# Folded groups 165 rows apart, small slots for the last raw rows, and a value test in flat parts, in a channel-attention kernel

## The chip, the cores and the metric

The kernel runs on one core of a Trainium2 chip. The metric is the device time of one execution in microseconds (us). Five engines take part: TensorE (PE, the sums), VectorE (DVE, bit work and scaling), ScalarE (ACT, the sigmoid, a range test, and the queue that issues all stores), SyncE (SP, the queue that issues all loads), and GpSimd (POOL, a fallback that does no work on these inputs). Loads and stores run on the core's 16 DMA engines.

## The reference

```python
H = W = 384
C = 384
x: (1, H, W, C) bf16, normal * 0.05        w1d: (1,) bf16

g = jnp.einsum("bhwc->bc", x) / (H * W)    # mean of each channel
s = sigmoid(g * w1d[0])                    # with k = 1
return x * s[:, None, None, :]
```

Each of the 384 channels is averaged over 147,456 positions, and the whole tensor (113 MB) is then scaled by one factor per channel. No output can be computed before every input has been read, and the tensor is larger than the core's own memory.

## The kernel before

The 147,456 positions are seen as 1152 "rows" of 128 partitions: one row is one position (384 channels, 768 bytes) in each of the 128 partitions, 98 KB in all.

**First pass.** SP loads all 1152 rows into one tile, `arena`, which has 275 row places. PE sums each row over the partitions by a matrix of ones (`sum_rows`, L227), all into one PSUM bank. 799 rows are "streamed": once PE has read them, their places are used again, and they are loaded a second time later. The other 353 rows are kept on the chip until they are scaled:

- 18 rows in PSUM (ACT copies them there, L315);
- 240 rows "folded" in four groups, `QS = [16, 16, 16, 12]`: of each group of 4q rows, q rows (called u) are loaded into the places `U`, 3q rows (called w) into the group's own area, and then the bits of u are put into the top exponent bits of w, so that 4q rows take 3q places;
- 95 rows raw, in `A`, `B`, `C`, `Y`, `U` and `T`, loaded last.

Before a group's w rows come, its area serves as a place for streamed rows; so do A, B and C.

**The fold** (`fold`, pieces of 4 rows of u and 12 of w; four pieces in groups 0 to 2, three in group 3). DVE makes four shifted copies of u in T (four instructions through the helper `bits`, L247), then writes the twelve w rows and the four u rows, masked and XORed, to Y for a range test (L247 again, one instruction for all of w, `three(ya, p)`, and one for u), then puts the copies into w (two through `join`, L253). The joins wait until PE has summed the rows that they change. ACT then reads Y in place and takes its sum into `seen` (L289). So the next piece's writes to Y wait for ACT, the next group's load into U waits for the last piece's reads of U, and the load of the raw rows into Y waits for ACT's last pass. If any tested value is out of range, `verdict` and `again` recompute the folded rows; on these inputs they do nothing.

**Order of the loads.** SP issues the loads in the order in which the program lists them, and a load that must wait for its place holds every later one. Before: the 18 rows, 523 streamed rows through all four areas, group 0, 72 streamed rows, group 1, 72, group 2, 72, group 3, 60, then the 95 raw rows.

**Second pass.** Once all 1152 rows are summed, ACT computes the factors (`s_bf`, L361). DVE scales what is on the chip (`scale`, L370), unfolds the groups (`unfold`), scales the PSUM rows (`from_psum`), and ACT's queue stores them; as places come free, SP loads streamed rows again, which are scaled and stored in turn. A loop at the end of the program plays this through with a row time of 0.2275 us and writes the instructions in the order in which it sees places come free. In the program a load waits for the stores that free its place, whatever the loop had assumed.

`Flow` collects all steps with the rows they read and write, and sets the waits from that; transfers of one queue share 24 semaphores, so that a transfer also waits for the one 24 before it.

Of the kernel before, what the change touches and what calls it, by code (L numbers as in the profile page):

```python
# [128 lines left out]
def kernel(  # L129
# [13 lines left out]
    B, H, W, C = x.shape  # L143
# [12 lines left out]
    base, areas = 0, []  # L156
# [1 line left out]
        areas.append((base, 3 * q))  # L158
        base += 3 * q
    RAW = {}  # L160
    for name, n in (("A", 16), ("B", 16), ("C", 15), ("Y", 16), ("U", 16), ("T", 16)):
        RAW[name] = (base, n)
        base += n
    ROWS = base
# [22 lines left out]
    def view(t, r0, n):  # L187
        return t[r0 * P : (r0 + n) * P, :].rearrange("(p r) c -> p r c", r=n)

    def rows(lo, n):  # L190
        return [("a", r) for r in range(lo, lo + n)]
# [5 lines left out]
    N_STREAM = RPP - kept  # L197
# [8 lines left out]
    c_raw = {}  # L206
# [8 lines left out]
    def load(chunk, a, lo=0, hi=None):  # L215

        r0, n = chunk
        hi = n if hi is None else hi
        fl.add(
            "SP",  # L220
            lambda: nc.sync.dma_start(out=arena[:, a : a + hi - lo, :], in_=view(xf, r0, n)[:, lo:hi, :]),  # L221
            writes=rows(a, hi - lo), dma=True,
        )

    def sum_rows(a, n):
        def emit(i, first, last):
            return nc.tensor.matmul(acc, lhsT=ones[:], rhs=arena[:, i, :], start=first, stop=last)  # L227

        for i in range(a, a + n):
            first, last = summed[0] == 0, summed[0] == RPP - 1  # L230
            fl.add(
                "PE", lambda i=i, f=first, l=last: emit(i, f, l),
                reads=[("a", i), "ones"], writes=["acc"],
            )
            summed[0] += 1

    def take(chunk, a):
        load(chunk, a)
        sum_rows(a, chunk[1])
# [4 lines left out]
    def bits(dst, src, op0, s0, op1, s1, reads, writes):  # L244
        fl.add(
            "DVE",
            lambda: nc.vector.tensor_scalar(out=dst, in0=src, scalar1=s0, scalar2=s1, op0=op0, op1=op1),  # L247
            reads=reads, writes=writes,
        )

    def join(dst, a, b, op, reads, writes):
        fl.add(
            "DVE", lambda: nc.vector.tensor_tensor(out=dst, in0=a, in1=b, op=op), reads=reads, writes=writes  # L253
        )

    def area(g, lo, p):
        a, n = areas[g]
        v = arena[:, a : a + n, :].rearrange("p (j q) c -> p j q c", j=3)[:, :, lo : lo + p, :]
        q = n // 3
        return v.bitcast(u16), [rows(a + j * q + lo, p) for j in range(3)]  # L260

    def flat(a, p):
        return arena[:, a : a + p, :].bitcast(u16)

    def three(a, p):
        return arena[:, a : a + 3 * p, :].rearrange("p (j q) c -> p j q c", j=3).bitcast(u16)

    SHL, SHR, AND, OR, XOR = (
        Op.logical_shift_left, Op.logical_shift_right, Op.bitwise_and, Op.bitwise_or, Op.bitwise_xor,
    )  # L270

    def fold(k):
        g, lo, p = pieces[k]
        w, wc = area(g, lo, p)
        wall = wc[0] + wc[1] + wc[2]
        ua, ta, ya = RAW["U"][0] + lo, RAW["T"][0], RAW["Y"][0]
        u, uc = flat(ua, p), rows(ua, p)
        for i, (op, by, mask) in enumerate(
            ((SHL, 4, 0x7800), (SHL, 8, 0x7800), (SHL, 12, 0x7000), (SHR, 4, 0x0800))
        ):  # L280
            bits(flat(ta + i * p, p), u, op, by, AND, mask, uc, rows(ta + i * p, p))
        bits(three(ya, p), w, AND, 0x7800, XOR, 0x3800, wall, rows(ya, 3 * p))
        bits(flat(ya + 3 * p, p), u, AND, 0x7800, XOR, 0x3800, uc, rows(ya + 3 * p, p))
        join(w, w, three(ta, p), XOR, wall + rows(ta, 3 * p), wall)
        join(w[:, 2], w[:, 2], flat(ta + 3 * p, p), XOR, wc[2] + rows(ta + 3 * p, p), wc[2])
        y = flat(ya, 4 * p)
        fl.add(
            "ACT",
            lambda: nc.scalar.activation(out=y, in_=y, func=ACTF.Copy, accum_out=seen[:, k : k + 1]),  # L289
            reads=rows(ya, 4 * p), writes=rows(ya, 4 * p) + [("seen", k)],  # L290
        )
# [12 lines left out]
    def stream(n, a):  # L304
        take((streamed[0], n), a)
        streamed[0] += n

    A, Bs, Cs, Y, U, T = (RAW[n][0] for n in "ABCYUT")
    take(c_ps, A)
    psflat = arena[:, A : A + PS, :].rearrange("p r c -> p (r c)")  # L310
    for i, bk in enumerate(banks):
        lo, hi = i * BANK, min((i + 1) * BANK, PS * C)
# [4 lines left out]
            ),  # L317
            reads=rows(A, PS), writes=[("bank", i)],
        )
    GAP = [(0, 48), (1, 12), (2, 12)]  # L320
    TAIL = [("A", 16), ("B", 16), ("C", 15), ("A", 13)]
    before = N_STREAM - 3 * 72 - sum(n for _, n in TAIL)
    i = 0
    while before:
        a, n = areas[i % 4]
        n = min(n, before)
        stream(n, a)
        before -= n
        i += 1
    k = 0  # L330
    for g, q in enumerate(QS):
        if g:
            a, n = areas[(g + 1) % 4] if g < 3 else areas[3]
            n = min(n, 48)
            if g < 3:
                stream(n, a)
            else:
                stream(n, a)
            rest = 72 - n
            stream(rest // 2, A)  # L340
            stream(rest - rest // 2, Bs)
        load(c_u[g], U)
        load(c_w[g], areas[g][0])
        sum_rows(U, q)
        sum_rows(areas[g][0], 3 * q)
        while k < len(pieces) and pieces[k][0] == g:
            fold(k)
            k += 1
    for name, n in TAIL:
        stream(n, RAW[name][0])  # L350
    assert streamed[0] == N_STREAM
    for name in "BCAYU":
        take(c_raw[name], RAW[name][0])
    for lo, hi in ((0, 8), (8, 12), (12, 14), (14, 15), (15, 16)):
        load(c_raw["T"], T + lo, lo, hi)
        sum_rows(T + lo, hi - lo)
    assert summed[0] == RPP

    fl.add(
# [143 lines left out]
    landed = deque()  # L503
    free = deque()
# [17 lines left out]
    def release(name):  # L522
        def f():
            if name in extra and extra[name]:
                extra[name] -= 1
                return
            free.append(RAW[name])
        return f

    for lo, hi in ((0, 1), (1, 2), (2, 4), (4, 8), (8, 16)):  # L530
        landed.append((c_raw["T"], T, lo, hi, None))
    for name in "ABCYU":
        n = RAW[name][1]
        landed.append((c_raw[name], RAW[name][0], 0, n, release(name)))
    unfolded = 0
    psum_done = False
    verdict_done = checked = False
# [3 lines left out]
    while True:  # L541

        if dve_at <= now:
# [9 lines left out]
            elif can:  # L553
                kk = unfolded
                g, lo, p = pieces[kk]
# [18 lines left out]
        while waiting and waiting[0][0] <= now:  # L574
            _, n, then = waiting.popleft()
# [5 lines left out]
        while free and todo[0] < N_STREAM and len(loads) < 6:  # L581
            a, n = free.popleft()
            n = min(n, N_STREAM - todo[0])
# [3 lines left out]
            cuts = list(range(0, n, 16)) + [n]  # L587
# [6 lines left out]
        for q in active:  # L594
            q[0][1] -= DT / len(active)
            if q[0][1] <= 0:
                then = q.popleft()[2]
# [41 lines left out]
```

## Time and profile before

| | |
|---|---|
| median of 3 runs | 793.52 us (793.11 to 794.05) |
| the profiled execution | 796.84 us, of which the span of the profile is 795.1 us |
| moved by DMA | 191.79 MB read, 113.25 MB written, 384 GB/s over the span |
| DVE busy | 466.6 us (59%) |
| PE busy | 226.5 us (28%), 1153 matmuls |
| ACT busy | 86.7 us (11%) |
| factors (`s_bf`) computed | at 332.6 us of the span |

The span is counted from the first to the last instruction of the profiled execution. Engine shares are averages over both passes; the first pass ends at 332.6 us, and PE has almost nothing to do after it. The chain of waits is followed back from the last instruction; in it, "SPq" is the load queue, "ACTq" the store queue.

### The profile page before, as it was taken

How to read it: one execution, taken by the hardware profiler on the slowest of the kernel's cores; microseconds unless marked ns; L12 is line 12 of the kernel's file. 1: busy time of each engine (PE TensorE's matmuls, PEld its weight loads, DVE VectorE, ACT ScalarE, POOL GpSimd, SP SyncE). 2: the span in 40 equal slices, each digit the busy share in tenths (PEclk: the TensorE clock that was granted, in tenths of full speed). 3: DMA queues.
4: the chain of work that ended last, by engine and by line, in shares of the span. 5: the costliest groups of instructions: out<-in, count | busy, mean ns of one | idle time of the engine just before them, and what ended most of it. 6: DMA issues, size and time to landing. Idle time of an engine off the chain costs nothing.

```text
span 795.1 us, 2991 instructions
## 1 busy us (share of the span) xinstructions
PE 226.5 (28%) x1153; PEld 122.2 (15%) x1153; DVE 466.6 (59%) x366; ACT 86.7 (11%) x39; POOL 0.2 (0%) x4
## 2 busy tenths in 40 slices
PE   2878888843837667500000000000000000000000
PEld 1444444421413333200000000000000000000000
DVE  0000000493782987299899938997599986374500
ACT  2000000252552555000000000000000000000000
POOL 0000000000000000000000000000000000000000
PEclk9898989875967889855555555555555555555555
DMA  9999999909559497699999999999999999999996
GB/s 356 433 428 437 422 441 428 402 5 411 212 210 419 182 391 312 261 362 426 425 425 430 432 421 429 432 411 420 425 426 422 423 428 428 425 433 432 425 430 296
DMA packets 28623, 305.25 MB, mean 384 GB/s; under 512 B 2880, under 2 KB 3648, under 8 KB 12096
## 3 DMA queue, kind: packets, MB, share of 16 engines
q1 hardware_dynamic: 11376, 191.80, 57.4%
q10 hardware_dynamic: 17232, 113.25, 34.1%
q8 instruction: 9, 0.15, 0.1%
q14 instruction: 6, 0.05, 0.0%
HBM read 191.79 MB, written 113.25 MB: 384 GB/s over the span
## 4 chain that ended last, share of the span: by engine, by line
DMA 51%; DVE 27%; PE 9%; ACT 5%; ACTq 2%; DVEq 0%; issue 0%; SPq 0%
DMA arena<-in_x_dram 27%; DMA out_dram<-arena 24%; DVE arena L370 10%; PE bank L227 9%; DVE arena L247 9%; ACT arena L289 5%; DVE arena L253 4%; DVE arena L404 2%; ACTq L380 2%; DVE arena L442 1%; DVEq L106 0%; SPq L221 0%; ACT s_bf L361 0%; SPq L634 0%; ACTq L112 0%
## 5 line engine op out<-in xcount | busy, mean ns | idle before, releaser
L247 DVE TENSOR_SCALAR arena<-arena 128x1536 uint16<-128x1536 uint16 x180 | 139.7, 821 | 199.1 <-DMA arena<-in_x_dram 150.0
L227 PE MATMUL bank<-arena,ones 128*128 128x384 bf16 x1152 | 226.3, 364 | 106.3 <-DMA arena<-in_x_dram 106.1
L370 DVE TENSOR_TENSOR arena<-arena,s_bf 128x6144 bf16<-128x6144 bf16 (+5 forms) x76 | 198.1, 2665 | 51.6 <-DMA arena<-in_x_dram 31.2
L227 PEld LDWEIGHTS bank<-arena,ones 128*128 128x128 bf16 x1152 | 122.1, 108 | 210.1 <-DMA arena<-in_x_dram 108.0
L253 DVE TENSOR_TENSOR arena<-arena 128x1536 uint16<-128x1536 uint16 (+1 forms) x75 | 95.4, 1272 | 20.9 <-PE bank L227 20.4
L289 ACT ACTIVATE arena<-arena 128x6144 uint16<-128x6144 uint16 x15 | 79.9, 5323 | 222.6 <-DVE arena L247 222.6
L404 DVE TENSOR_TENSOR arena<-arena,s_bf 128x4608 bf16<-128x4608 bf16 x15 | 38.3, 2552 | 0.0
L463 PE MATMUL bank<-odd,ones 128*128 128x1 bf16 x1 | 0.2, 186 | 31.0 <-DVE odd L458 31.0
L298 DVE TENSOR_SCALAR w_sc<-w_bf 128x1 f32<-128x1 bf16 x1 | 0.2, 153 | 14.8 <-DMA w_bf<-in_w1d_dram 14.8
L442 DVE TENSOR_TENSOR arena<-bank,s_bf 128x768 bf16<-128x768 bf16 (+2 forms) x15 | 5.0, 390 | 0.1
L463 PEld LDWEIGHTS bank<-odd,ones 128*128 128x128 bf16 x1 | 0.1, 104 | 31.3 <-DVE odd L458 31.3
L315 ACT COPY bank<-arena 128x512 uint32<-128x512 uint32 (+1 forms) x7 | 3.6, 566 | 5.9 <-DMA arena<-in_x_dram 5.9
L289 ACT ACTIVATION_READ_ACCUMULATOR arena<-arena 128x1 f32 x15 | 2.8, 186 | 0.0
L361 ACT ACTIVATE s_bf<-bank,w_sc 128x384 bf16<-128x384 f32 x1 | 0.6, 582 | 17.2 <-PE bank L227 17.2
L607 ACT ACT_TABLE_LOAD x1 | 1.3, 1283 | 0.7 <-PEq L623 0.7
L295 DVE MEMSET ones<- 128x128 bf16 x1 | 0.2, 165 | 1.0 <-SPq L106 1.0
L467 DVE CAST odd_i<-bank 128x1 int32<-128x1 f32 x1 | 0.2, 158 | 0.3 <-PE bank L463 0.3
L458 DVE TENSOR_SCALAR odd<-worst 128x1 bf16<-128x1 f32 x1 | 0.2, 157 | 0.0
L453 DVE TENSOR_REDUCE worst<-seen 128x1 f32<-128x15 f32 x1 | 0.2, 161 | 0.0
L623 POOL MEMSET const-bfloat16-1.0<- 128x1 bf16 x1 | 0.1, 102 | 0.0
L623 POOL MEMSET const-uint8-127<- 128x1 uint8 x1 | 0.1, 101 | 0.0
L623 POOL MEMSET const-float32-0.0<- 128x1 f32 x1 | 0.1, 99 | 0.2 <-issue 0.2
(1 smaller groups left out, 0.1 us busy)
## 6 DMA issues: line engine op xcount, KB each, us to landing
arena<-in_x_dram SPq DMA_DIRECT2D x21, 4608.0 KB, 20.7
out_dram<-arena ACTq DMA_DIRECT2D x48, 1536.0 KB, 30.7
arena<-in_x_dram SPq DMA_DIRECT2D x29, 1536.0 KB, 11.8
arena<-in_x_dram SPq DMA_DIRECT2D x5, 3456.0 KB, 26.1
out_dram<-arena ACTq DMA_DIRECT2D x15, 1152.0 KB, 27.8
arena<-in_x_dram SPq DMA_DIRECT2D x8, 1440.0 KB, 11.5
out_dram<-arena ACTq DMA_DIRECT2D x7, 1440.0 KB, 22.8
arena<-in_x_dram SPq DMA_DIRECT2D x5, 1728.0 KB, 7.0
```

Source lines behind the costliest of these rows:

```text
L227: return nc.tensor.matmul(acc, lhsT=ones[:], rhs=arena[:, i, :], start=first, stop=last)
L247: lambda: nc.vector.tensor_scalar(out=dst, in0=src, scalar1=s0, scalar2=s1, op0=op0, op1=op1),
L253: "DVE", lambda: nc.vector.tensor_tensor(out=dst, in0=a, in1=b, op=op), reads=reads, writes=writes
L289: lambda: nc.scalar.activation(out=y, in_=y, func=ACTF.Copy, accum_out=seen[:, k : k + 1]),
L315: lambda bk=bk, lo=lo, hi=hi: nc.scalar.copy(bk[:, 0 : hi - lo].bitcast(u32), psflat[:, lo:hi].bitcast(u32)),
L361: lambda: nc.scalar.activation(out=s_bf[:], in_=acc, func=ACTF.Sigmoid, scale=w_sc[:, 0:1]),
L370: lambda: nc.vector.tensor_tensor(out=v, in0=v, in1=s_bf[:, None, :].to_broadcast([P, n, C]), op=Op.mult),
L380: lambda: nc.scalar.dma_start(out=view(of, r0, n)[:, lo:hi, :], in_=arena[:, a : a + hi - lo, :]),
L404: lambda: nc.vector.tensor_tensor(out=wv, in0=wv, in1=s_bf[:, None, None, :].to_broadcast([P, 3, p, C]), op=Op.mult),
L442: lambda sv=sv, dv=dv, by=by: nc.vector.tensor_tensor(out=dv, in0=sv, in1=by, op=Op.mult),
L463: lambda: nc.tensor.matmul(votes, lhsT=ones[:], rhs=odd[:], start=True, stop=True),
L607: nc.scalar.preload_act_table(ACTF.Sigmoid)
```

## The change

Three things are edited. Nothing that is computed changes, and the numbers of streamed, folded and raw rows are the same.

1. **Spacing.** 225 streamed rows come before group 0, 165 between one group and the next (72 before), and 79 after group 3 (60 before). The streamed rows go in pieces of half an area, 24 or 18 rows (48 or 36 before). Between groups they take the areas that hold no folded group yet, and the small slots.
2. **Small slots.** A, B and C become one stretch A of 47 rows, cut into six slots of 8 rows (the last of 7). The last streamed rows and the raw rows are loaded slot by slot, and in the second pass each slot is stored, freed and loaded again by itself. The raw rows that are scaled first are those of the first slot (1, 1, 2 and 4 rows), where before they were T's.
3. **Test in flat parts.** The instruction that writes all twelve w rows of a piece to Y becomes three, one for each stretch of four rows.

```diff
-    for name, n in (("A", 16), ("B", 16), ("C", 15), ("Y", 16), ("U", 16), ("T", 16)):
+    for name, n in (("A", 47), ("Y", 16), ("U", 16), ("T", 16)):
...
-        bits(three(ya, p), w, AND, 0x7800, XOR, 0x3800, wall, rows(ya, 3 * p))
+        for j in range(3):
+            bits(flat(ya + j * p, p), w[:, j], AND, 0x7800, XOR, 0x3800, wc[j], rows(ya + j * p, p))
...
-    GAP = [(0, 48), (1, 12), (2, 12)]
-    TAIL = [("A", 16), ("B", 16), ("C", 15), ("A", 13)]
-    before = N_STREAM - 3 * 72 - sum(n for _, n in TAIL)
-    i = 0
-    while before:
-        a, n = areas[i % 4]
-        n = min(n, before)
-        stream(n, a)
-        before -= n
-        i += 1
+    def stream_all(n, where):
+        i = 0
+        while n:
+            a, m = where[i % len(where)]
+            m = min(n, m)
+            stream(m, a)
+            n -= m
+            i += 1
+
+    def halves_of(*gs):
+        return [(areas[g][0] + h * areas[g][1] // 2, areas[g][1] // 2) for g in gs for h in (0, 1)]
+
+    SMALL = [(A + i, min(8, Y - A - i)) for i in range(0, Y - A, 8)]
+    BEFORE = [
+        (N_STREAM - 79 - 3 * 165, halves_of(1, 2, 3)),
+        (165, halves_of(1, 2, 3) + SMALL),
+        (165, halves_of(2, 3) + SMALL + halves_of(3) + SMALL),
+        (165, halves_of(3) + SMALL * 9),
+    ]
     k = 0
     for g, q in enumerate(QS):
-        if g:
-            a, n = areas[(g + 1) % 4] if g < 3 else areas[3]
-            n = min(n, 48)
-            if g < 3:
-                stream(n, a)
-            else:
-                stream(n, a)
-            rest = 72 - n
-            stream(rest // 2, A)
-            stream(rest - rest // 2, Bs)
+        stream_all(*BEFORE[g])
         load(c_u[g], U)
         load(c_w[g], areas[g][0])
...
-    for name, n in TAIL:
-        stream(n, RAW[name][0])
+    stream_all(79, SMALL)
     assert streamed[0] == N_STREAM
-    for name in "BCAYU":
-        take(c_raw[name], RAW[name][0])
+    first = 4
+
+    def take_part(name, lo, hi):
+        load(c_raw[name], RAW[name][0] + lo, lo, hi)
+        sum_rows(RAW[name][0] + lo, hi - lo)
+
+    for a, n in SMALL[first:] + SMALL[:first]:
+        take_part("A", a - A, a - A + n)
+    for name in "YU":
+        take_part(name, 0, 16)
...
-    for lo, hi in ((0, 1), (1, 2), (2, 4), (4, 8), (8, 16)):
-        landed.append((c_raw["T"], T, lo, hi, None))
-    for name in "ABCYU":
-        n = RAW[name][1]
-        landed.append((c_raw[name], RAW[name][0], 0, n, release(name)))
+    for j, (a, n) in enumerate(SMALL):
+        lo = a - A
+        cuts = [lo, lo + 1, lo + 2, lo + 4, lo + n] if not j else [lo, lo + n]
+        for e, f in zip(cuts, cuts[1:]):
+            then = (lambda a=a, n=n: free.append((a, n))) if f == lo + n else None
+            landed.append((c_raw["A"], A, e, f, then))
+    landed.append((c_raw["T"], T, 0, 8, None))
+    landed.append((c_raw["T"], T, 8, 16, None))
+    for name in "YU":
+        landed.append((c_raw[name], RAW[name][0], 0, 16, release(name)))
```

What this does to the order of the instructions, at three places. In the rows, 384 elements of a partition are one row, so 128x18432 is a load of 48 rows.

The load queue (SP) from group 0 to group 1, before: U and the w rows of group 0, streamed rows, U of group 1 (waiting for DVE), its w rows.

```order
L221 DMA arena<-in_x_dram 128x6144
L221 DMA arena<-in_x_dram 128x18432 [waits f_PE] x2
L221 DMA arena<-in_x_dram 128x4608 [waits f_ACT]
L221 DMA arena<-in_x_dram 128x4608
L221 DMA arena<-in_x_dram 128x6144 [waits f_DVE]
L221 DMA arena<-in_x_dram 128x18432
```

The same stretch after the change:

```order
L221 DMA arena<-in_x_dram 128x6144
L221 DMA arena<-in_x_dram 128x18432
L221 DMA arena<-in_x_dram 128x9216 [waits f_PE] x4
L221 DMA arena<-in_x_dram 128x6912 x2
L221 DMA arena<-in_x_dram 128x3072 [waits f_ACT]
L221 DMA arena<-in_x_dram 128x3072 x3
L221 DMA arena<-in_x_dram 128x384
L221 DMA arena<-in_x_dram 128x6144 [waits f_DVE]
L221 DMA arena<-in_x_dram 128x18432 [waits f_PE]
```

The load that waits for DVE now stands behind 165 streamed rows instead of 72 (48 + 12 + 12).

The load queue from group 3's U to the raw rows in T, before:

```order
L221 DMA arena<-in_x_dram 128x4608 [waits f_DVE]
L221 DMA arena<-in_x_dram 128x13824
L221 DMA arena<-in_x_dram 128x6144
L221 DMA arena<-in_x_dram 128x6144 [waits f_PE]
L221 DMA arena<-in_x_dram 128x5760 [waits f_PE]
L221 DMA arena<-in_x_dram 128x4992 [waits f_PE]
L221 DMA arena<-in_x_dram 128x6144 [waits f_PE]
L221 DMA arena<-in_x_dram 128x5760 [waits f_PE]
L221 DMA arena<-in_x_dram 128x6144 [waits f_PE]
L221 DMA arena<-in_x_dram 128x6144 [waits f_ACT]
L221 DMA arena<-in_x_dram 128x6144
L221 DMA arena<-in_x_dram 128x3072 [waits f_DVE]
```

and after the change:

```order
L221 DMA arena<-in_x_dram 128x4608 [waits f_DVE]
L221 DMA arena<-in_x_dram 128x13824
L221 DMA arena<-in_x_dram 128x3072 [waits f_PE] x5
L221 DMA arena<-in_x_dram 128x2688
L221 DMA arena<-in_x_dram 128x3072 [waits f_PE] x5
L221 DMA arena<-in_x_dram 128x2688 [waits f_PE]
L221 DMA arena<-in_x_dram 128x3072 [waits f_PE] x4
L221 DMA arena<-in_x_dram 128x6144 [waits f_ACT]
L221 DMA arena<-in_x_dram 128x6144
L221 DMA arena<-in_x_dram 128x3072 [waits f_DVE]
```

The 107 rows in pieces of 13 to 16 ahead of Y (the load that waits for ACT) are now 126 rows in pieces of 7 or 8, each waiting for PE to have read the slot.

DVE at the first piece of group 0, before (after two instructions of the start):

```order
L295 MEMSET ones 128x128
L298 TENSOR_SCALAR w_sc<-w_bf 128x1
L247 TENSOR_SCALAR arena<-arena 128x1536 x4
L247 TENSOR_SCALAR arena<-arena 128x4608
L247 TENSOR_SCALAR arena<-arena 128x1536
L253 TENSOR_TENSOR arena<-arena 128x3x1536
L253 TENSOR_TENSOR arena<-arena 128x1536
```

and after the change:

```order
L296 MEMSET ones 128x128
L299 TENSOR_SCALAR w_sc<-w_bf 128x1
L247 TENSOR_SCALAR arena<-arena 128x1536 x8
L253 TENSOR_TENSOR arena<-arena 128x3x1536
L253 TENSOR_TENSOR arena<-arena 128x1536
```

The wide instruction of 4608 elements is now three of 1536, so that eight equal ones stand in a row.

More of the change, by code (lines that the diff above doesn't have):

```diff
@@ L306, in stream @@
         streamed[0] += n
-    A, Bs, Cs, Y, U, T = (RAW[n][0] for n in "ABCYUT")
+    A, Y, U, T = (RAW[n][0] for n in "AYUT")
     take(c_ps, A)
@@ L348 @@
             k += 1
-    for name, n in TAIL:
-        stream(n, RAW[name][0])
+    stream_all(79, SMALL)
     assert streamed[0] == N_STREAM
-    for name in "BCAYU":
-        take(c_raw[name], RAW[name][0])
+    first = 4
[6 more added lines that the diff above has]
+        take_part(name, 0, 16)
     for lo, hi in ((0, 8), (8, 12), (12, 14), (14, 15), (15, 16)):
-        load(c_raw["T"], T + lo, lo, hi)
-        sum_rows(T + lo, hi - lo)
+        take_part("T", lo, hi)
     assert summed[0] == RPP
```

## The prediction

> **What bounds the kernel now.** I read the 40 slices first, then who held the load queue, then the chain that ended last, then stretches of it.
>
> ```profile
> PEclk9898989875967889855555555555555555555555
> DMA  9999999909559497699999999999999999999996
> GB/s 356 433 428 437 422 441 428 402 5 411 212 210 419 182 391 312 261 362 426 425 425 430 432 421 429 432 411 420 425 426 422 423 428 428 425 433 432 425 430 296
> HBM read 191.79 MB, written 113.25 MB: 384 GB/s over the span
> ```
>
> The transfers set the pace nearly everywhere: some 430 GB/s in slices 2 to 7 and from slice 19 on. In between, in slices 9 to 18 (159 to 358 us), they drop out, down to 5 GB/s. Those holes lie in the first pass, where the sum must be complete before anything is stored.
>
> ```profile
> SPq L221 <- PE bank L227: 226.9, 17, 34.7
> SPq L221 <- DVE arena L247: 62.5, 3, 42.4
> SPq L221 <- ACT arena L289: 9.1, 1, 9.1
> ```
>
> Of what the load queue (SP) waited for in the first 333 us, the long PE row is harmless: SP had run ahead and data were still queued. The three waits on DVE are the loads into U, which the fold before must have read; the one on ACT is the load into Y. The chain shows what they cost:
>
> ```profile
> 144.21 8.96 PE bank L227 x36
> ...
> 175.53 3.03 DVE arena L247 x2
> 178.58 0.33 SPq L221
> ...
> 195.90 8.72 PE bank L227 x36
> ...
> 230.04 0.33 SPq L221
> ...
> 247.37 8.58 PE bank L227 x36
> ...
> 272.87 0.33 SPq L221
> ...
> 286.58 6.47 PE bank L227 x28
> ...
> 309.96 5.43 ACT arena L289 x2
> 315.41 6.23 DMA arena<-in_x_dram
> 321.64 0.05 issue
> 321.68 10.92 PE bank L227 x48
> 332.60 0.02 issue
> 332.63 0.59 ACT s_bf L361
> ```
>
> PE starts on the w rows of groups 0 to 3 when they land: 144.21, 195.90, 247.37, 286.58. To price holes I need the time of one row (one row per partition, 98 KB):
>
> ```profile
> 62.40:103.36 40.96, 34.30 (x180) 18.86 (x180) 0.00 (x0) 0.00 (x0) 0.00 (x0) 0.88 1.00 431
> 103.36:144.17 40.81, 34.14 (x179) 18.79 (x179) 1.97 (x4) 0.00 (x0) 0.00 (x0) 0.88 1.00 431
> 144.00:150.00 6.00, 5.79 (x19) 2.75 (x20) 3.02 (x2) 2.75 (x1) 0.00 (x0) 0.50 1.03 442
> 150.00:166.00 16.00, 15.98 (x98) 9.41 (x97) 12.73 (x13) 7.08 (x3) 0.00 (x0) 0.99 0.51 213
> 400.00:500.00 100.00, 0.00 (x0) 0.00 (x0) 83.24 (x69) 0.00 (x0) 0.00 (x0) 0.50 1.01 427
> ```
>
> Columns: length, busy time with instruction counts of PE, PE's weight loads, DVE, ACT, POOL, then granted clock, DMA share, GB/s. The first two give (40.96 + 40.81) / 359 = 0.2278 us of DMA per row. The next two give PE: 0.31 us per row at clock 0.50, 0.163 at 0.99. So PE is slower than the DMA when cold and faster when warm.
>
> Now the holes. After group 0's w rows only 72 rows stand ahead of U's next load: 16.4 us, so the queue is dry at 160.6. U is released at 178.58, and the next 64 rows (14.6 us) have landed at 195.90, so they began at 181.3: **20.7 us** idle. Likewise 195.90 + 16.4 = 212.3 against 247.37 - 14.6 = 232.8: **20.5**. Then 263.8 against 286.58 - 10.9 (48 rows) = 275.7: **11.9**. After group 3, 155 rows would need 35.3 us, to 321.9, and the sum is done at 332.6: **10.7** (the wait for Y, and PE's tail of 48 rows from a cold clock). Together 63.8 us.
>
> **The change part by part.** *165 rows between groups.* It adds no bytes. By the order of the loads, the 165 rows are out of SP's hands before U's next load is due, except where a slot repeats (below), so they last 165 x 0.2278 = 37.6 us after the w rows. Before, U's release came 178.58 - 144.21 = 34.4 us after them. Release to landing of 16 rows was 6.23 us (the Y row), less 3.64 of transfer: 2.6 us of latency. Even at the old fold speed 34.4 + 2.6 = 37.0 just fits. So the three DVE holes, 53.1 us, go; behind the waiting load stand the w rows and all later loads, and nothing of those is needed earlier.
>
> *Test in flat parts.* One instruction over three parts becomes three over one part each.
>
> ```profile
> L247 DVE TENSOR_SCALAR arena<-arena 128x1536 uint16<-128x1536 uint16 x150 | 76.7, 554 | 171.0 <-DMA arena<-in_x_dram 123.1 <-DMA out_dram<-arena 47.4
> L247 DVE TENSOR_SCALAR arena<-arena 128x4608 uint16<-128x4608 uint16 x30 | 64.5, 2151 | 28.1 <-DMA arena<-in_x_dram 26.9
> ```
>
> And from the chain, an unfolding in the second pass:
>
> ```profile
> 379.01 1.40 DVE arena L247 x3
> ...
> 382.75 1.67 DVE arena L247
> ...
> 388.25 0.97 DVE arena L370
> ```
>
> The 30 wide ones are of two kinds: the 15 in the second pass took 1.67 us each, going by the one in the chain, so the 15 of the fold took (64.5 - 25.1) / 15 = 2.63. Three flat ones are 3 x 0.554 = 1.66: 0.97 less per piece. A piece's period was ACT 5.43 + DVE 3.03 = 8.5 us, both on the Y rows; it becomes 5.43 + 4 x 0.554 = 7.6. U's release, three periods on, comes at 34.4 - 2.7 = 31.7 us: 31.7 + 2.6 = 34.3 of 37.6, 3.3 us to spare.
>
> *Small slots.* The last streams go through 47 rows in six slots of 8 (7). A slot can be refilled only when PE has read it, and PE is still on the 48 w rows when they land. After group 2: PE needs 10.92 us for 48 rows from cold (row at 321.68), 36 rows of area 3 x 0.163 = 5.9, the first slot 1.3: 18.1, with 2.6 of latency 20.7. The queue holds 36 + 47 rows = 18.9 us: **1.8** idle. After group 3: 36 rows take 6.47 + 8 x 0.163 = 7.8, the slot 1.3, latency 2.6: 11.7 against 47 rows = 10.7: **1.0**. Once warm, PE frees a slot every 1.3 us and the DMA fills one in 1.82, so there is no further loss. Groups 0 and 1 have 165 and 131 rows of slots and lose nothing.
>
> *The end.* Y's load came 315.41 - 286.58 = 28.8 us after group 3's w rows; two shorter periods make it 27.0, plus 2.6 = 29.6. Ahead stand 79 + 47 rows = 28.7 us, plus the 1.0 above: even, I take **0.5**. After U lands PE has 16 + 16 warm rows, 5.2 us, while T's rows need 3.6: a tail of **1.6** instead of the wait and the 10.9.
>
> *More transfers.* Loads go from 79 to 136, stores from 92 to 112, by count of the order. Their issue (0.33 us on SP, the chain's row) hides behind 1.8 us of transfer. Their fixed time hides behind what is queued; unhidden, 77 x 2.6 = 200 us. The stretch 400 to 500 is the nearest row:
>
> ```profile
> out_dram<-arena ACTq DMA_DIRECT2D x6, 1152.0 KB, 17.3
> ...
> out_dram<-arena ACTq DMA_DIRECT2D x6, 384.0 KB, 16.8
> ```
>
> These are of its 29 transfers, six of only 384 KB, and it moved 427 GB/s. I take 0. The Trainium skill (DMA: Bandwidth & Descriptors, Bandwidth) asks for 1 MiB or more per transfer and has 341 GB/s at 1 MB against 425 at 16 MB; by its fixed 2.0 us (Anatomy of one DMA), 77 transfers would be an estimated 154 us. The quoted stretch does not agree for transfers in a filled queue.
>
> *Second pass.* The same 191.8 MB; 795.1 - 333.2 = 461.9 us now. Its start is weak:
>
> ```profile
> 335.00:340.00 5.00, 0.00 (x0) 0.00 (x0) 5.00 (x3) 0.00 (x0) 0.00 (x0) 0.79 0.76 295
> ```
>
> The page's slice 18 (338 to 358) shows 362 GB/s where 427 is normal. Before, the first reload waits for 32 rows to be stored, now for 8, so I take **-2 us**. Bounds: -4 (the whole weakness) and +20 (two stops of an unfolding's 10 us each, by 379.01 to 389.22 above). For the upper: T, which the first unfolding writes, is now stored behind 47 other rows; against it, Y and U (32 rows, 7.3 us) are queued behind T, and reloads run.
>
> Sum: 63.8 holes leave, 1.8 + 1.0 + 0.5 + 1.6 = 4.9 come, -2: -60.9. Span 795.1 - 60.9 = 734.2. The profiled execution took 796.84, 1.7 more than its span, and the runs' median 793.52, 3.3 less than that: 734.2 + 1.7 - 3.3 = **733 us**.
>
> **The rivals.** *The second pass gives part back.* DVE needs T, U and Y free in another order, and small slots tie each reload to one store. For it: DVE is 83% busy in 400 to 500 and has waited 47.4 us on stores (the row of 150). Against: 427 GB/s all the same, so the queue has depth. Price 10 to 22 us: 743 to 757.
>
> *The fold is still late.* If the flat parts gain nothing and PE's rows lie later, U's release slips past 37.6 us; the old speed has 0.6 to spare. Each further 5 us costs up to 15 over three groups, with the end up to 25: about 755.
>
> *Small transfers bare their fixed time (other side).* In the ring of small slots each load would start only when the one before is done. From 63.8 / 77 = 0.8 us unhidden per added transfer the gain is gone; at the full 2.6 us it is 200 - 61 = 139 slower, 930. Against it: six slots against a turn of 1.8 + 1.3 + 2.6 = 5.7 us, 10.7 around the ring.
>
> The 1 MiB rule of the Trainium skill, above, would act here in this way.
>
> *PE stays cold (also the other side).* 1152 rows x 0.31 = 357 us for the sums alone, 24 past the 333 at which they are done now: about 820. It needs pauses long enough to cool. Rows with short ones:
>
> ```profile
> 303.67 2.29 PE L227 MATMUL bank<-arena,ones 128*128 128x384 bf16 x13 [1.70 <-DMA arena<-in_x_dram]
> 307.35 2.77 PE L227 MATMUL bank<-arena,ones 128*128 128x384 bf16 x16 [1.39 <-DMA arena<-in_x_dram]
> ...
> 321.68 3.70 PE L227 MATMUL bank<-arena,ones 128*128 128x384 bf16 x11 [4.12 <-DMA arena<-in_x_dram]
> ```
>
> After 1.70 and 1.39 us it ran at 0.17 per row, after 4.12 at 0.34. A 24-row piece leaves it 24 x (0.228 - 0.163) = 1.6 us.
>
> **How the numbers follow.** Forecast 0.75, its own range 727 to 742; the second pass gives back 0.15; the fold is late 0.05; bare transfers 0.02, cold PE 0.01; nothing moves 0.02. From 724 (no new holes, no Y wait, 4 us won at the second start, and 0.4% for this run against others, as 796.84 stands to 793.52) to 756 about 0.86 lie inside. A run can be told from no change at about 0.2%, 1.6 us: faster 0.95, same 0.02, slower 0.03.
>
> **What would show it.** The DMA row at 9 without a break from slice 2 to the end of the first pass; the three waits of SP on DVE still there, but the GB/s beside them above 400; the s_bf step near 275 us instead of 332.6; two dips of 1 to 2 us, 19 and 11 us after the w rows of groups 2 and 3; from s_bf to the end 458 to 462. Below 400 GB/s in a ring stretch speaks for the bare transfers, a clock of 0.5 there for the cold PE, and an end more than 465 us after s_bf for the give-back.

## The result, and the profile after

The changed kernel takes **747.18 us** (median of 4 runs, 745.43 to 748.78), against 793.78 us for the kernel before in the same comparison: a ratio of 0.9407, with a 95% interval of 0.9376 to 0.9439. It is 46.6 us faster; 60.5 were forecast. The time lies inside the range on record (724 to 756) and 14.2 us above the forecast of 733. Its profiled execution took 746.17 us, with a span of 744.3.

From here on "before" is the kernel before and "after" the changed one. First the slices of after and what it moved:

```profile
DMA  8999999999999988999999999999999999999996
GB/s 344 423 430 434 429 416 430 424 425 431 370 413 423 370 334 335 427 355 427 422 422 431 421 423 425 442 405 425 425 435 412 427 419 426 427 428 445 405 432 271
HBM read 191.79 MB, written 113.25 MB: 410 GB/s over the span
```

The slices with 5, 212, 210 and 182 GB/s are gone, and the same bytes go through at 410 GB/s over the span instead of 384. What is left are shallow places: slice 11, slices 14 to 16 and slice 18, counted from 1 as in the prediction. The load queue's waits up to 300 us:

```profile
SPq L221 <- PE bank L227: 163.0, 42, 25.6
SPq L221 <- DVE arena L247: 28.6, 2, 22.0
SPq L221 <- ACT arena L290: 4.1, 1, 4.1
```

SP still waits for ACT once, and for DVE twice where it waited three times before. A wait of the issuing queue costs nothing while data are still queued. The chain has the times:

```profile
76.72 7.71 PE bank L227 x36
...
106.67 0.33 SPq L221
...
129.43 8.64 PE bank L227 x36
...
160.32 0.33 SPq L221
...
182.28 22.13 PE bank L227 x124
...
213.59 0.33 SPq L221
...
233.81 6.36 PE bank L227 x28
...
260.43 0.33 SPq L221
...
278.30 0.59 ACT s_bf L368
...
292.39 16.83 DMA out_dram<-arena
```

The w rows of the four groups landed at 76.72, 129.43, 182.28 and 233.81. For groups 1 and 2, U was released 29.95 and 30.89 us after the landing before it, well before the 37.6 us of queued rows ran out. For group 3 it was not U that held the queue: DVE's last instructions on U ended at 212.3, and SP stood at a small slot that PE freed at 213.59, 31.31 us after group 2's w rows. The stretches between those landings, and the two weak places in them (columns as in the prediction):

```profile
76.72:129.43 52.71, 40.05 (x230) 22.38 (x230) 29.13 (x40) 21.67 (x8) 0.00 (x0) 0.92 1.01 426
129.43:182.28 52.85, 40.51 (x229) 22.93 (x230) 29.16 (x40) 21.66 (x8) 0.00 (x0) 0.92 1.01 426
182.28:233.81 51.53, 40.26 (x225) 21.72 (x225) 29.16 (x40) 21.67 (x8) 0.00 (x0) 0.93 0.98 401
233.81:278.30 44.49, 37.84 (x210) 20.07 (x210) 19.93 (x26) 16.25 (x7) 0.00 (x0) 0.96 0.93 370
198.00:206.00 8.00, 8.00 (x51) 4.79 (x49) 7.82 (x11) 5.97 (x3) 0.00 (x0) 1.00 0.85 303
242.00:250.00 8.00, 8.00 (x51) 4.83 (x50) 7.93 (x11) 2.46 (x1) 0.00 (x0) 1.00 0.89 300
```

Groups 0 and 1 now run with no hole at all. After groups 2 and 3 there is a dip of eight us each at some 300 GB/s, in which PE is busy without a break. The factors are ready at 278.30 instead of 332.63. The start of the second pass is the last place to compare, three times 20 us from the factors on, after and then before:

```profile
278.90:298.90 20.00, 0.00 (x0) 0.00 (x0) 19.99 (x14) 0.00 (x0) 0.00 (x0) 0.57 0.88 336
298.90:318.90 20.00, 0.00 (x0) 0.00 (x0) 11.81 (x12) 0.00 (x0) 0.00 (x0) 0.50 0.96 402
318.90:338.90 20.00, 0.18 (x1) 0.10 (x1) 19.51 (x32) 0.00 (x0) 0.00 (x0) 0.50 1.01 387
```

```profile
333.20:353.20 20.00, 0.00 (x0) 0.00 (x0) 19.96 (x11) 0.01 (x1) 0.00 (x0) 0.62 0.82 303
353.20:373.20 20.00, 0.19 (x1) 0.10 (x1) 19.30 (x17) 0.00 (x0) 0.00 (x0) 0.50 1.00 426
373.20:393.20 20.00, 0.00 (x0) 0.00 (x0) 16.53 (x28) 0.00 (x0) 0.00 (x0) 0.50 1.02 432
```

The first 20 us gained (336 against 303), the next 40 lost more. The chain above points at the store of T, 16.83 us from the end of its scaling at 292.39 to its landing, before which DVE can't unfold anything. For the first half of that time DVE still scaled other rows, up to 300.56; then it stood still twice, 8.1 us together:

```profile
305.65 0.56 DVE L247 TENSOR_SCALAR arena<-arena 128x1536 uint16<-128x1536 uint16 x1 [5.09 <-DMA out_dram<-arena]
309.24 1.03 DVE L247 TENSOR_SCALAR arena<-arena 128x1536 uint16<-128x1536 uint16 x2 [3.03 <-DMA out_dram<-arena]
```

From the factors to the end it takes 465.4 us, 3.5 more than before.

### The profile page after: what moved, and what is told of

Same layout as the page of the kernel before. It is cut to its first block, busy times and chain, and to the rows that moved or that the text cites. A ratio compares the mean times of both kernels' runs of the same rounds, so it can differ in the third digit from the quotient of the medians.

```text
span 744.3 us, 3123 instructions
## 1 busy us (share of the span) xinstructions
PE 207.5 (28%) x1153; PEld 113.5 (15%) x1153; DVE 452.1 (61%) x416; ACT 86.7 (12%) x39; POOL 0.2 (0%) x4
## 4 chain that ended last, share of the span: by engine, by line
DMA 51%; DVE 27%; PE 8%; ACT 4%; another core or an unknown queue 4%; SPq 1%; DVEq 0%; issue 0%
DMA arena<-in_x_dram 26%; DMA out_dram<-arena 24%; DVE arena L377 11%; DVE arena L247 8%; PE bank L227 8%; DVE arena L253 5%; ACT arena L290 4%; DVE arena L411 3%; DVE arena L449 1%; SPq L221 1%; DVEq L106 0%; ACT s_bf L368 0%; PE bank L470 0%; DVE odd L465 0%
## 5 line engine op out<-in xcount | busy, mean ns | idle before, releaser
L247 DVE TENSOR_SCALAR arena<-arena 128x1536 uint16<-128x1536 uint16 (+1 forms) x210 | 123.9, 639 | 177.1 <-DMA arena<-in_x_dram 112.9
L227 PE MATMUL bank<-arena,ones 128*128 128x384 bf16 x1152 | 207.3, 340 | 70.9 <-DMA arena<-in_x_dram 70.9
L377 DVE TENSOR_TENSOR arena<-arena,s_bf 128x3072 bf16<-128x3072 bf16 (+5 forms) x96 | 199.2, 2140 | 38.8 <-ACT s_bf L368 20.5
L227 PEld LDWEIGHTS bank<-arena,ones 128*128 128x128 bf16 x1152 | 113.3, 101 | 164.5 <-DMA arena<-in_x_dram 79.0
## 6 DMA issues: line engine op xcount, KB each, us to landing
arena<-in_x_dram SPq DMA_DIRECT2D x10, 1728.0 KB, 34.4
```

What stands on the lines that cost most here:

```text
L377: lambda: nc.vector.tensor_tensor(out=v, in0=v, in1=s_bf[:, None, :].to_broadcast([P, n, C]), op=Op.mult),
```

## The experiments

**The theory** after these readings: the distance between the groups made the gain; the flat test only adds reserve; the two dips come from PE still being on a w load when the small slots should be refilled; the second pass loses by T's late store. **The rivals**: the faster test makes the gain; the small transfers themselves cost what is missing, in the ring and everywhere; the second pass takes longer for a reason that has nothing to do with T. There were eleven runs, the last of them the changed kernel again.

**The flat test alone, in the kernel before.**

```diff
-        bits(three(ya, p), w, AND, 0x7800, XOR, 0x3800, wall, rows(ya, 3 * p))
+        for j in range(3):
+            bits(flat(ya + j * p, p), w[:, j], AND, 0x7800, XOR, 0x3800, wc[j], rows(ya + j * p, p))
```

> The kernel before with the test in flat parts alone (72 rows between groups, large slots). Theory, the holes are the time by which U's release comes after the streamed rows: a piece's period falls from 8.5 to about 7.5 us, so each of the three releases comes three periods on, 2.9 us earlier, and Y's load two periods, 2 us earlier: 10 us in all, 783 to 785 us; the three releases 31 to 32 us after the w rows instead of 34.4. Rival, the holes are set by something else (the number of loads, the clock of PE): within 2 us of 793.8.

Measured: 784.84 us, ratio 0.9886 (0.9863 to 0.9909). Its chain:

```profile
144.07 7.72 PE bank L227 x36
...
159.14 5.42 ACT arena L290 x2
...
166.59 5.42 ACT arena L290 x2
...
174.03 0.33 SPq L221
```

One period is 166.59 - 159.14 = 7.45 us, and U comes free 29.96 us after the w rows instead of 34.4. That shortens every hole and closes none: some 9 of the 47 us, as expected.

**The change without the flat test** (the diff above backwards, in after).

> The changed kernel with the wide test instruction of before. Theory: U's release at 34.4 us plus 2.6 of latency is 37.0 against 165 rows that last 37.6 to 38.0, so no hole opens between groups; only Y's load comes 2 us later: 747 to 750 us, DMA in the stretches between groups still at 420 GB/s or more. Rival, the 165 rows suffice only with the faster fold: three holes of 2 to 4 us and the end, 756 us or more.

Measured: 748.70 us, ratio 0.9419 (0.9397 to 0.9441). Its chain has the long periods back (102.59 - 94.09 = 8.5 us):

```profile
76.73 8.95 PE bank L227 x36
...
94.09 5.42 ACT arena L289 x2
...
102.59 5.43 ACT arena L289 x2
...
111.09 0.33 SPq L221
```

U comes free 34.4 us after the w rows, still ahead of the 37.6, and there is no hole. So the two gains don't add: with the distance the flat parts are worth about 2 us at the end (factors at 280.25 against 278.30), and the medians differ by 1.5, less than their intervals can tell. (Its profiled execution, 742.42 us, is the fastest of its five.)

**120 rows between the groups** (after, the other 135 rows ahead of group 0).

```diff
-        (N_STREAM - 79 - 3 * 165, halves_of(1, 2, 3)),
-        (165, halves_of(1, 2, 3) + SMALL),
+        (N_STREAM - 79 - 3 * 120, halves_of(1, 2, 3)),
+        (120, halves_of(1, 2, 3) + SMALL),
```

(and the two lines after it alike)

> The changed kernel with 120 rows between groups instead of 165 (the others go ahead of group 0). Theory: 120 rows last 27.7 us, U's release comes at 30 to 31 us, landing starts 2.6 later, so three holes of 5 to 6 us: 760 to 765 us, the holes seen in the GB/s about 28 us after the w rows of groups 0 to 2. Rival, small pieces and not the distance bring the gain: 747 us.

Measured: 756.12 us, ratio 0.9505 (0.9469 to 0.9541), 9 us slower than after, 4 to 9 less than expected. PE's row of time shows the queue run dry:

```profile
144.00 4.93 PE L227 MATMUL bank<-arena,ones 128*128 128x384 bf16 x16 [6.15 <-DMA arena<-in_x_dram]
...
191.43 5.11 PE L227 MATMUL bank<-arena,ones 128*128 128x384 bf16 x16 [6.83 <-DMA arena<-in_x_dram]
```

The U rows of groups 1 and 2 (16 each) land at 144.00 and 191.43. Group 0's w rows landed at 107.67; 120 rows last 27.7 us from there at 426 GB/s, to 135.4, and U's 16 rows (3.6 us) began at 140.4: a hole of 5 us. The next, worked out alike, is also 5 us. The third is only about 2, and there the stretch up to group 3's w rows loses no more than in after (2.7 us against 3.0, by rows at 0.2278 us), since after has its dip in that place. So the distance decides, with the size that row time and release give, and two more holes than in after are left: the factors came at 288.30, 10.0 us later.

**T stored right behind the first small slot** (after).

```diff
         for e, f in zip(cuts, cuts[1:]):
             ...
+        if not j:
+            landed.append((c_raw["T"], T, 0, 8, None))
+            landed.append((c_raw["T"], T, 8, 16, None))
-    landed.append((c_raw["T"], T, 0, 8, None))
-    landed.append((c_raw["T"], T, 8, 16, None))
```

> The changed kernel with T's rows scaled and stored right behind the first small slot instead of behind all six. Theory, the second pass lost time because the first unfolding waits for T's store, which stands behind 47 rows and the reloads: VectorE's wait of 16.8 us at the start of the second pass shrinks below 8, the GB/s 30 to 60 us after the factors rise from 370-400 to 420, and 2 to 4 us are won: 743 to 745 us. Rival, the weak start comes from stores without reloads and the count of small transfers: no change, 746 to 748.

Measured: 746.13 us, ratio 0.9396 (0.9379 to 0.9414). From the factors on:

```profile
280.00:300.00 20.00, 0.00 (x0) 0.00 (x0) 19.98 (x14) 0.00 (x0) 0.00 (x0) 0.56 0.89 332
300.00:320.00 20.00, 0.19 (x1) 0.11 (x1) 15.92 (x18) 0.00 (x0) 0.00 (x0) 0.50 1.01 426
```

DVE no longer waits for a store here; it waits 3.7 us for two reloads instead. (The 16.8 us of the expectation were the store's whole way; the wait was 8.1.) The second 20 us carry 426 GB/s instead of 402, the next 422, and the first 4 less than in after. That is worth (24 + 35 - 4) x 20 / 428 = 2.6 us of transfer. The median fell by only 1.0 us, which the intervals do not tell from nothing, so the rates came as the theory had them and the time as the rival had it. The second pass took 462.6 us in its profiled execution.

**The w rows in three loads** (after): each a third of the area, so that PE can begin when the first has landed.

```diff
-        load(c_w[g], areas[g][0])
+        for j in range(3):
+            load(c_w[g], areas[g][0] + j * q, j * q, (j + 1) * q)
```

> The changed kernel with the w rows of a group in three loads (16 or 12 rows) instead of one, so that PE sums them while they land. Theory: the two dips in the small ring (198 to 206 and 242 to 248 us, together about 4.3 us of DMA time) come from PE starting 48 or 36 rows late; with parts PE is one part behind, the first slot is free long before the queue is dry, the dips vanish, and U and Y are released 4 to 6 us earlier: the factors at 273 to 275 us instead of 278.3, 742 to 744 us. Rival, the dips are the latency of small transfers themselves: the factors stay at 277 to 279, 746 to 748 us.

Measured: 745.05 us, ratio 0.9382 (0.9368 to 0.9397). The rings after groups 2 and 3:

```profile
195.00:220.00 25.00, 20.24 (x112) 9.62 (x110) 14.02 (x19) 12.31 (x6) 0.00 (x0) 1.00 1.02 416
235.00:259.00 24.00, 18.23 (x100) 8.56 (x99) 16.35 (x22) 14.68 (x6) 0.00 (x0) 1.00 1.02 417
```

In after both stretches ran at 381. Both dips are gone with smaller transfers in greater number, so PE's late start was their cause and not the transfers. The factors came at 275.71, 2.6 earlier than in after, but a little later than expected, and the median lies a microsecond above the expectation. The ring's 416 is still not 431, with the DMA engines at full share.

**Loads of 48 and 36 rows again** (after; `halves_of` gives whole areas) and **slots of 16 rows** (after, three slots instead of six).

```diff
-        return [(areas[g][0] + h * areas[g][1] // 2, areas[g][1] // 2) for g in gs for h in (0, 1)]
+        return [areas[g] for g in gs]
```

> The changed kernel with streamed rows in whole areas (48 or 36 rows a load) instead of halves. Theory, the first pass ran at 425 to 429 GB/s instead of 431 because its loads are smaller: 431 in the stretch before group 0 and 1 to 2 us less until the factors. Rival, the lower rate comes from the folds that now run beside the loads: 425 between groups as before. Against both, PE pauses up to 4 us between loads of 48 rows and restarts at half clock (clock below 0.9 in that stretch), which costs time only if it comes too late for the small slots. 744 to 749 us.

```diff
-    SMALL = [(A + i, min(8, Y - A - i)) for i in range(0, Y - A, 8)]
+    SMALL = [(A + i, min(16, Y - A - i)) for i in range(0, Y - A, 16)]
-    first = 4
+    first = 2
-        cuts = [lo, lo + 1, lo + 2, lo + 4, lo + n] if not j else [lo, lo + n]
+        cuts = [lo, lo + 1, lo + 2, lo + 4, lo + 8, lo + n] if not j else [lo, lo + n]
```

> The changed kernel with three slots of 16 (15) rows instead of six of 8 (7). Theory: the rows behind groups 2 and 3 wait for PE to read 16 rows instead of 8, 1.3 us more in each of the two dips, so the factors come 2 to 4 us later (280 to 282); the second pass keeps its length within the scatter: 748 to 752 us. Rival, small transfers are themselves slow: 16-row slots win 3 us or more, 744 or less.

Measured: 747.48 us, ratio 0.9399 (0.9378 to 0.9420), and 745.43 us, ratio 0.9388 (0.9350 to 0.9425). Neither differs from after. First the kernel with whole areas, and below it the second dip of the unedited kernel in its other profiled execution (the last run of this section):

```profile
20.00:76.00 56.00, 43.74 (x241) 24.45 (x241) 1.96 (x4) 0.00 (x0) 0.00 (x0) 0.93 1.00 432
```

```profile
242.00:250.00 8.00, 8.00 (x51) 4.83 (x50) 7.31 (x11) 0.55 (x3) 0.00 (x0) 1.00 0.68 216
```

With whole areas the streams run at 432 in 20 to 76 us, where after has 429. Their second dip is deeper than after's, 215 GB/s in 242 to 250 us against 300, but this can't be put down to the edit: the unedited kernel had 216 when it was profiled again. PE took 7.55 us for the first 28 of group 3's w rows there, at a granted clock of 0.62, and 6.36 at 0.74 in after, and the factors came at 280.92 instead of 278.30. So the first pass alone varies by 2.6 us from one execution to another. Then the kernel with slots of 16:

```profile
200.00:205.00 5.00, 5.00 (x32) 3.03 (x31) 4.82 (x10) 3.36 (x2) 0.00 (x0) 1.00 0.63 204
207.00:230.00 23.00, 16.32 (x94) 8.71 (x94) 11.03 (x16) 9.23 (x4) 0.00 (x0) 1.00 1.02 433
```

In the same two stretches after has 302 and 430: the dip is deeper here, and what follows hardly differs. In 207 to 220 us alone, before group 3's rows, it is 429 against 420. Here 748 to 752 us were expected, with the factors at 280 to 282. They came at 279.45, and the second pass took 462.3 us, within the spread of that stage.

**T early and the w rows in parts** (after with both edits), and **the same with slots of 16** (three edits).

> The changed kernel with both edits: w rows in three loads, and T stored behind the first small slot. Theory: both gains add, the factors at 273 to 275 us and the second pass at 462 to 463 us plus the scatter of its last stores: 739 to 743 us. Rival, what one wins the other's stretch gives back: 745 or more.

> The changed kernel with w rows in three loads, T stored behind the first small slot, and three slots of 16 (15) rows instead of six of 8. Theory: with the dips gone by the parts, what is left of the first pass is the rate of 8-row loads (416 GB/s in the ring of small slots, 431 to 433 with 16-row slots): the ring stretches at 430, the factors 2 to 3 us earlier than with parts alone (272 to 274 us instead of 275.7), 738 to 742 us. Rival, with 16-row slots the ring of three is too short even for a PE that keeps up, and the dips come back: 743 or more.

Measured: 742.55 us, ratio 0.9343 (0.9319 to 0.9366), and **737.10 us, ratio 0.9286 (0.9259 to 0.9312)**. The first is 2.5 us faster than the kernel with the w rows in parts, measured in the same comparison, and the two intervals do not meet, though single executions overlap; its factors came at 275.88, a little later than expected and no earlier than in parts alone, so the 2.5 us are the early store's. (The two profiled executions don't show it, with 461.6 us of second pass each; that of the w rows in parts is the fastest of its six.) The second kernel is faster than both, about a microsecond below its expectation. Its rows:

```profile
195.00:220.00 25.00, 18.23 (x106) 9.64 (x104) 13.62 (x19) 11.91 (x6) 0.00 (x0) 1.00 1.00 413
275.10:295.10 20.00, 0.00 (x0) 0.00 (x0) 20.00 (x12) 0.00 (x0) 0.00 (x0) 0.59 0.89 338
295.10:315.10 20.00, 0.18 (x1) 0.10 (x1) 19.55 (x25) 0.00 (x0) 0.00 (x0) 0.50 1.01 429
```

The factors come at 274.49, about where the forecast had them, and the second pass takes 460.9 us. The ring was expected at 430 and stays at 413 all the same: it moved 429 GB/s from 185 to 195 us and 403 from 200 to 207, with the DMA engines at full share in both. Why was not settled.

**All four edits** (with whole areas too), and **after once more, unedited**, on the same chip as the kernel with three edits.

> As the run before, and streamed rows in whole areas of 48 or 36 rows. Theory: 432 instead of 429 GB/s before group 0 and 427 to 429 instead of 425 between groups, another 1 to 2 us: 737 to 741 us. Rival: PE, 48 rows late and cold after pauses of 4 us, brings back the dips in the small slots: 742 or more.

> The changed kernel once more, unedited, so that the two runs before stand beside it on the same chip, and to see how the length of its second pass scatters from one profile to another: 745 to 749 us; the second pass within 460 to 467 us.

Measured: 741.15 us, ratio 0.9318 (0.9291 to 0.9344), and 748.86 us, ratio 0.9419 (0.9387 to 0.9451). Whole areas bring the dip back:

```profile
200.00:205.00 5.00, 5.00 (x33) 3.04 (x31) 4.82 (x10) 3.34 (x2) 0.00 (x0) 1.00 0.52 169
```

With 48-row pieces PE is behind again when the ring starts, and of the 4 us that the median lost, 3 lie in s_bf at 277.49 instead of 274.49; the two intervals overlap. Against after in the same comparison, the kernel with three edits is 748.86 - 737.10 = 11.8 us faster. By the profiled executions 6.4 of that lie in the first pass (280.92 against 274.49) and 5.7 in the second (466.6 against 460.9).

## Why the prediction was right, and where it was off

**The holes: right.** 63.8 us were to leave, since 165 rows outlast U's release. They left; the release was even earlier than forecast (29.95 and 30.89 us for the first two groups, against 31.7). The sign "the three waits of SP on DVE still there" did not come as said: the third was a wait for PE at a small slot. That the distance does it, at either speed of the fold, is shown by the runs with the wide test (no hole at 34.4 us) and with 120 rows (holes of 5 us).

**The flat parts: right.** 0.97 us per piece were forecast. The wide ones left over, 15 in the second pass, show what the fold's had cost:

```profile
L247 DVE TENSOR_SCALAR arena<-arena 128x4608 uint16<-128x4608 uint16 x15 | 26.3, 1751 | 0.0
```

Of the 64.5 us before, 26.3 belong to them, so the fold's fifteen took (64.5 - 26.3) / 15 = 2.55 us each, against 3 x 0.554: 0.89 us saved. These times overlap a little where instructions follow each other (four flat ones take 1.98 us in the chain, not 4 x 0.554 = 2.2), so the chain is the better measure: DVE's part of a period went from 3.03 to 1.98 us, 1.05 saved, and the period from 8.5 to 7.45, where 7.6 was forecast.

**The first pass: 4.6 us too short.** By the sum, s_bf would have started at 332.63 - 63.8 + 4.9 = 273.7; it was 278.3. A ledger by stretches, at the forecast's 0.2278 us per row: up to group 1's and then group 2's landing 229 rows should take 52.2 us each and took 52.7 and 52.9; with 0.4 up to group 0's (76.72, where 298 rows fewer than before give 144.21 - 67.9 = 76.3), the streams lost 1.6. From there to group 3's landing 213 rows should take 48.5 and took 51.5: 3.0, where a dip of 1.8 was in the sum. The last stretch lost 4.8, where 3.1 was (dip, Y, tail). So two terms were mis-sized:

- *More transfers*, put at 0. The 24-row pieces ran at 429, the streams beside the folds at 426, the 8-row ring at 416 when no dip disturbed it, against 431 for the 48-row loads before: 3% in the ring, about 1% elsewhere. Ahead of group 0 the size of the loads is the reason, since whole areas gave 432 there. In the ring the evidence is divided (429 against 420 with slots of 16, but 413 with three edits), and beside the folds whole areas gave between 422 and 428, so the cause is not shown in these two places. The quoted stretch of the second pass could not show it, since small and large transfers were mixed there. The Trainium skill (DMA: Bandwidth & Descriptors, Bandwidth) has the direction right, 768 KB loads being slower than larger ones, but not the size: it gives 341 GB/s for 1 MB, measured on transfers that GpSimd issues, and these, smaller, issued by SP and kept queued, had 416.
- *Small slots*, put at 1.8 and 1.0. The mechanism held, as the loads of w in parts showed, but the dips cost 8 x (1 - 303/425) = 2.3 and 8 x (1 - 300/425) = 2.4 us (2.7 and 3.9 in after once more, at 283 and 216 GB/s). They are not the one short stop of the sum: PE did free the first slot about when the sum said (a load went out at 199.22, 16.9 us after the w rows), and after that the rate stayed low until PE had caught up at 207, six us in which the sum had "no further loss".

**The wait for Y: right.** Its load went out 26.6 us after group 3's w rows (27.0 forecast). The tail was 2.0 instead of 1.6 us.

**The second pass: -2 was the wrong sign.** 459.9 us were forecast and 465.4 came, just past the 465 that the prediction had named as the sign of the give-back. The step that failed is the argument that against T's late store "Y and U (32 rows, 7.3 us) are queued behind T, and reloads run": DVE had to stop for 8.1 us, while only the first 20 us gained. By the three windows of 20 us, after moved (1161 - 1125) x 20 / 428 = 1.7 us of transfer less than before in the same time, instead of 2 more. The transfers filled most of the stop, so the price was far below the 10 us per stop that the rival had reckoned.

That the late store costs this is shown. In the other five profiled executions that have it behind six small slots (the wide test, 120 rows, w in parts, whole areas, after once more), the same three windows add up to 1127 to 1144; in the two that have T stored early behind such slots, to 1180 and 1182, some 2.5 us of transfer more. The kernels with w in parts, 745.05 and 742.55 us, say the same in their total. The other 1.8 us of the 5.5 lie in the spread of this stage: the same second pass, T's late store included, took 459.8 to 466.9 us in the six profiled executions.

**The profile's time against the median: 4.5 us.** The sum was made against a profiled execution 3.3 us above the median of its runs, and these 3.3 were taken off again. That correction does not carry over: the profiled execution of after lay 1.0 us below its median, and 1.9 instead of 1.7 above its span. So 4.6 + 5.5 + 4.5 = 14.6 us from the sum's 732.6, which had been rounded up to 733.

**The rivals.** The fold was not late. A ring stretch below 400 GB/s was to speak for the bare transfers, and after had 381 in 195 to 220 us; but with PE on time the same small loads ran at 416, so it was the dips. PE didn't stay cold, its granted clock being 0.92 to 0.96 in the four stretches from landing to landing and to the factors:

```profile
46.05 9.62 PE L227 MATMUL bank<-arena,ones 128*128 128x384 bf16 x48 [2.08 <-DMA arena<-in_x_dram]
118.50 2.77 PE L227 MATMUL bank<-arena,ones 128*128 128x384 bf16 x16 [2.30 <-DMA arena<-in_x_dram]
129.43 10.74 PE L227 MATMUL bank<-arena,ones 128*128 128x384 bf16 x49 [8.15 <-DMA arena<-in_x_dram]
```

After a pause of 2.30 us a row took 0.17 us, after 8.15 us 0.22 on the mean of 49. The Trainium skill (TensorE: Matmul & The Clock Gate, Part 1) puts the fall to half clock behind an idle window of about 3.4 us, and these rows agree only in part. Past the start, only the loads of w leave PE a pause beyond that; but after one of 2.08 us, at 46.05, the granted clock was 0.62 for the next 4.45 us. So a shorter pause can be enough; why it was there, and not after 2.30 us or, in the run with the wide test, after 2.71, is open.

## What to carry to other kernels

A load that waits for its place is free as long as the rows queued ahead of it outlast the release plus the latency of the restart; work both out in row times and set the distance from them, and the speed of the work behind the release then hardly matters. When such a hole is closed, look at who is late next: here a consumer that got 48 rows at once was still behind when small slots wanted refilling, and handing it the rows in three loads took the dips away, and showed clearly in the total only together with an earlier store, and more with larger slots as well. Don't carry the offset between one profiled execution and a median over into a forecast.

## What the runs showed of the hardware

- In the dips data were queued, yet they moved at 300 GB/s: from 199.22 to 205.6 six loads of 8 or 7 rows (4.6 MB) went out, and from 200 to 206 us, at 304 GB/s, only 1.8 MB moved. Why few fresh small loads run below the rate of a long queue was not settled.
- The second pass starts at 303 to 338 GB/s in its first 20 us in all kernels whose windows are shown, with the DMA engines 82 to 89% busy, and reaches 420 to 430 later. Why was not tried beyond the size of the first slot.
- The last transfers end unevenly. Rows of the last 10 us, after and then the run with the wide test:

```profile
734.30:739.30 5.00, 0.00 (x0) 0.00 (x0) 0.00 (x0) 0.00 (x0) 0.00 (x0) 0.50 0.59 246
739.30:744.30 5.00, 0.00 (x0) 0.00 (x0) 0.00 (x0) 0.00 (x0) 0.00 (x0) 0.50 0.06 26
```

```profile
730.60:735.60 5.00, 0.00 (x0) 0.00 (x0) 0.00 (x0) 0.00 (x0) 0.00 (x0) 0.50 1.01 429
735.60:740.60 5.00, 0.00 (x0) 0.00 (x0) 0.00 (x0) 0.00 (x0) 0.00 (x0) 0.50 0.32 130
```

With the same second pass, after moved (246 + 26) x 5 = 1360 KB there and the other 2795 KB, 1435 KB or 3.4 us at 427 GB/s apart. A share of the scatter between executions is made in these last microseconds.
